# The opening of a windowed-attention and MoE kernel: two loads by SyncE in f32, a new order, normalisations on two engines

## The chip, the cores and the metric

The kernel runs on one NeuronCore of a Trainium2 chip. The metric is the device time of one execution in microseconds (us); lower is better. The core has five engines, each with its own queue of instructions that it works through in order: TensorE (PE, matmuls and weight loads), VectorE (DVE), ScalarE (ACT), GpSimd (POOL) and SyncE (SP, which only issues DMAs here). DMAs are moved by 16 DMA engines that all queues share. A DMA that POOL issues can change the type on the way (f32 to bf16); those that SP issues here keep it.

## The reference

```python
# q, k, v: [8, 8, 576, 64] f32
scores = scale * np.matmul(q, k.transpose(0, 1, 3, 2))
rel = pos[:, None] - pos[None, :]
mask = (rel >= 0) & (rel < 64)
scores = np.where(mask, scores, -1000000000.0)
attn = softmax(scores)                       # over the last axis
x = (attn @ v) laid out as [4608, 512]       # tokens x (heads x 64)
h = x @ w_in                                 # [512, 2048]
g = h * np.cos(h)
out = g @ w_out                              # [2048, 512]
```

Each token attends to itself and the 63 before it in its sequence. The result goes through a two-layer block with the gate h * cos(h).

## The kernel before

The 4,608 tokens are cut into 9 MoE tiles of 512 tokens. A tile's `h` is computed in 16 blocks of 128 features (4 matmuls of 512 columns each, L421), ACT takes the sine (cos(h) is sin(h + pi/2)), DVE multiplies (L549), and 4 blocks of 128 tokens of the result are summed over 16 matmuls each (L560). Attention for later tokens runs between these matmuls. All that is scheduled by hand: the program's order on each engine is the order in which the Python code emits its instructions.

Attention works on units (b, p, j): batch b, pair p of heads (two heads fill the 128 partitions), block j of 64 queries. Up to four units make a group. A group passes through these steps:

- load (`load_heads` L159: one pair of heads of q or k, 128 x 576, by POOL with a cast to bf16), transposes on PE through the identity (`transposed` L197, 18 matmuls of 64x64), and a copy from PSUM to `qT` or `kT` (`put_q` L217, `put_k` L242, DVE or ACT);
- scores (`g_scores` L262, PE; the first eight groups add the mask by a matmul with `mask16`, L270), the row maximum (`g_max` L292, DVE), the exponential with its sum (`g_exp` L304, ACT, four instructions of 128 columns), the reciprocal of the sum (`g_inv`, DVE, L318), the normalised weights `w` (`g_norm` L321, a product on POOL or DVE, L325);
- transposes of `w` (`g_trans` L328, on PE, or by a DMA of SP), their copy to `wT` (`g_put` L340), the product with v (`values_half` L364 for the first tile), the copy to `xT` (`put_x_half` L375).

`v` is needed with two alignments, so half of it is copied within SBUF (`spread_v` L180, by DVE, POOL, or a DMA of SP).

The opening, until the first tiles are under way, is the string `FIRST` (L47): a list of steps separated by blanks, which a loop (L524) emits one after the other. A step's first part names a function (the table `steps`, L505), the numbers are its arguments, and a last letter names the engine: d DVE, a ACT, p POOL, s SP. A number at the end of a step that writes PSUM picks one of five banks (`BANKS`, L121). The ones that matter here:

- `Lq0.p`, `Lk0.p`: load pair p of batch 0; `Lq1`, `Lk1` of batch 1; `Lv0`, `Lv1` chunks of v; `Lwi`, `Lwo` quarters of `w_in` and `w_out`. All of them are issued by POOL;
- `tq.p`, `tk.p` transposes and `pq.p`, `pk.p` copies of batch 0; `Tq`, `Tk`, `Pq`, `Pk` of batch 1;
- `s.p.g`, `m.p.g`, `e.p.g`, `i.p.g`, `n.p.g`, `w.p.g`, `c.p.g`: scores, maximum, exponential, reciprocal, normalisation, transposes and copy of group g of pair p; `Gs`, `Gm`, ... the same for later groups by their number;
- `v.a.g` and `x.a.g`: values and xT copy for pairs 2a, 2a+1 of half g of the first tile. `h.g.f`: 8 matmuls of 256 columns of the first tile's half g (`first_half` L380), `S` the sine, `g` the gate; `o` the second layer;
- `ms.i`: clear one of the eight `qB` tiles; `io`: an iota on POOL; `id`: the identity made from it on DVE (L138); `mk`: the masks on DVE (L140 to L149); `mc`: their cast on ACT; `zA`, `zB`, `zC`, `y`: pieces of `spread_v`; `tb`: ACT's table for the sine.

POOL's loads use eight semaphores in turn, so that each load waits for the landing of the one eight loads earlier; a load that waits holds up what stands behind it on POOL, products (`n...p`) among it. `h.0.0`, the first MoE matmuls, need `x.0.0` and `x.1.0`, and these need all four pairs' groups of half 0.

Of the kernel before, what the change touches and what calls it, by code (L numbers as in the profile page):

```python
# [10 lines left out]
def _safe_warn(msg, *a, **kw):  # L11
# [3 lines left out]
F32 = mybir.dt.float32  # L15
BF16 = mybir.dt.bfloat16
AF = mybir.ActivationFunctionType
ALU = mybir.AluOpType
# [18 lines left out]
RC = 9  # L37
PAIRS = 4
# [6 lines left out]


FIRST = (  # L47
# [21 lines left out]
)  # L69


# [1 line left out]
def kernel(  # L73
# [9 lines left out]
    nc = tc.nc  # L83
    B, H, S, D = q.shape
    assert (B, H, S, D) == (8, 8, 576, 64)
    scale = 1.0 / math.sqrt(D)
    d_model = H * D
# [10 lines left out]
    moe = ctx.enter_context(tc.tile_pool(name="moe", bufs=2))  # L98
# [10 lines left out]
    ident = const.tile([128, 128], BF16, name="ident")  # L109
    mask = const.tile([128, 3, 128], F32, name="mask")  # L110
# [4 lines left out]
    st = {}  # L115

    H_BANKS = [banks * 3 + ("X0",) for banks in (("O1", "X0", "X1", "S", "O0"), ("X0", "X1", "O1", "S", "O0"))]
    S_BANKS = ("X1", "S", "X0")  # L120
    BANKS = ("O1", "X0", "X1", "S", "O0")  # L121
    W_PARTS = 4
# [2 lines left out]
    def bank(which, name):  # L125
        return ps.tile([128, 512], F32, tag=which, name=name)

    def copy(engine, out, in_):
        {"a": nc.scalar.copy, "p": nc.gpsimd.tensor_copy}.get(engine, nc.vector.tensor_copy)(out, in_)  # L129
# [1 line left out]


    def put_steps():
        nc.gpsimd.iota(mask.rearrange("p u c -> p (u c)")[:, 0:192], pattern=[[1, 192]], base=0, channel_multiplier=-1,
                       allow_small_or_imprecise_dtypes=True)

    def put_ident():
        nc.vector.tensor_scalar(ident, mask[:, 0], 0.0, 1.0, ALU.is_equal, ALU.mult)  # L138

    def put_masks():  # L140
        steps = mask.rearrange("p u c -> p (u c)")
        for h in range(2):
            nc.vector.tensor_scalar(mask[64 * h:64 * h + 64, 2], steps[64 * h:64 * h + 64, 64 * h:64 * h + 128],
                                    2.0, -65.0, ALU.mult, ALU.add)
        nc.vector.tensor_tensor(out=mask[:, 2], in0=mask[:, 2], in1=mask[:, 2], op=ALU.mult)
        nc.vector.tensor_scalar(mask[:, 1], mask[:, 2], 64.0 ** 2, NEG, ALU.is_gt, ALU.mult)
        nc.vector.tensor_scalar(mask[:, 2], mask[:, 1], -1.0, NEG, ALU.mult, ALU.add)
        nc.vector.tensor_copy(mask[:, 0, 0:64], mask[:, 2, 0:64])
        nc.vector.memset(mask[:, 0, 64:128], NEG)  # L149
# [6 lines left out]
    def rows_tile(name):  # L156
        return ld.tile([128, NC * H * D], BF16, tag=name, name=name)

    def load_heads(name, b, p0=0, n=PAIRS):  # L159
        if (name, b) not in st:  # L160
            st[name, b] = rows_tile(name)[:, 0:PAIRS * RC * D].rearrange("p (a x) -> p a x", a=PAIRS)
        src = {"q": q, "k": k}[name][b, 2 * p0:2 * p0 + 2 * n]
        nc.gpsimd.dma_start(out=st[name, b][:, p0:p0 + n],
                            in_=src.rearrange("(a h) (p c) d -> (h p) a (c d)", h=2, c=RC))

    def load_chunk(name, b, c):
        if (name, b) not in st:
            st[name, b] = rows_tile(name)[0:NP].rearrange("p (c x) -> p c x", c=NC)
        src = {"q": q, "k": k}[name][b, :, c * NP:c * NP + NP]
        nc.gpsimd.dma_start(out=st[name, b][:, c].rearrange("p (h d) -> p h d", h=H),  # L170
                            in_=src.rearrange("h p d -> p h d"))
# [246 lines left out]
    def first(mt, ff, ks, start, stop):  # L418
        if start:
            st["h", ff] = bank(H_BANKS[mt == 1][ff], "h_ps")  # L420
        nc.tensor.matmul(out=st["h", ff], lhsT=w_in_sb[:, ks, ff * 128:ff * 128 + 128],  # L421
# [35 lines left out]
    n = n_listed  # L457
# [35 lines left out]
            at(time + 0.2 + 0.1 * p, put_x, mt, p, "a" if p == 1 else None)  # L493


    nc.vector.memset(small, 0.0)
    exp_table()

# [3 lines left out]
    def spread_first(lo, hi):  # L502
        return lambda i, engine: spread_v(0, i, engine, lo, hi)

    steps = {"Lq0": lambda p: load_heads("q", 0, p, 1), "Lk0": lambda p: load_heads("k", 0, p, 1),  # L505
             "Lq1": lambda p: load_heads("q", 1, p, 1), "Lk1": lambda p: load_heads("k", 1, p, 1),
             "Lv0": lambda c: load_v(0, c), "Lv1": lambda c: load_v(1, c), "Lq2": lambda c: load_chunk("q", 2, c), "Lk2": lambda c: load_chunk("k", 2, c),
             "Lwi": lambda i: load_w_in(i * d_ff // W_PARTS, (i + 1) * d_ff // W_PARTS),
             "Lwo": lambda i: load_w_out(i * n_ff // W_PARTS, (i + 1) * n_ff // W_PARTS),
             "io": put_steps, "id": put_ident, "mk": put_masks, "mc": cast_masks, "ms": clear_first,  # L510
             "tq": lambda p: tr_q(0, p), "tk": lambda p: tr_k(0, p), "Tq": lambda p: tr_q(1, p), "Tk": lambda p: tr_k(1, p),
             "pq": lambda p, engine: put_q(0, p, engine), "pk": lambda p, engine: put_k(0, p, engine),
             "Pq": lambda p, engine: put_q(1, p, engine), "Pk": lambda p, engine: put_k(1, p, engine),
# [16 lines left out]
    for mt in range(1, n_mt):  # L530
        base = mt * T
# [4 lines left out]
        for ff in range(n_ff):  # L536
# [8 lines left out]
            e = ff % 2  # L545
# [5 lines left out]
        for ms0 in range(0, MT // 128, 2):  # L551
            o_sb = moe.tile([128, 2, d_model], F32, tag="out", name="out_sb", bufs=2)
            o_ps = [bank(which, "out_ps") for which in (("O1",) if mt == n_mt - 1 and ms0 else ("O1", "O0"))]
            for e in range(2):
                ms = ms0 + e
# [44 lines left out]
```

## Time and profile before

| what | us |
|---|---|
| median of 3 runs | 317.94 (317.11 to 318.19) |
| the profiled execution's own time | 319.05 |
| its span (first to last instruction) | 317.3 |
| first transposes on PE | 4.53 |
| first exponential on ACT | 8.68 |
| first MoE matmul (L385) | 25.03 |
| PE busy in the span | 300.3 |

The profile is of one execution. Its times count from the first instruction. PEclk is the share of the TensorE clock that was granted. The timeline merges neighbouring instructions of one kind (x4: four of them) and gives in brackets how long the engine stood idle before, and what ended that.

The loads of the opening are issued by POOL from 1.25 us on and land one behind the other: q of the first pair (issued at 1.25) took 3.2 us to land, the next q (2.85) 4.5, the first quarter of w_in (12.93) 7.8 us.

### The profile page before, as it was taken

What the parts mean: (1) busy time and instruction counts of PE and PEld (TensorE: products, weight loads), DVE (VectorE), ACT (ScalarE), POOL (GpSimd) and SP (SyncE); (2) the same over time, 40 slices, a digit from 0 to 9 for tenths busy, and PEclk for the clock granted to TensorE, in tenths of its full rate; (3) what the DMA queues carried; (4) which work ended last, traced back from release to release, by engine and by line L of the source; (5) the groups of instructions that cost most, each with busy time, mean ns of one, the idle gap of its engine ahead of it and who ended that gap; (6) DMA issues with size and microseconds to landing.
All of it is one profiled execution on the core that took longest, in us unless ns stands there. A gap on an engine that the chain in (4) does not pass through costs nothing.

```text
span 317.3 us, 7950 instructions
## 1 busy us (share of the span) xinstructions
PE 300.3 (95%) x2627; PEld 163.4 (51%) x2659; DVE 233.4 (74%) x879; ACT 236.5 (75%) x784; POOL 192.7 (61%) x226
## 2 busy tenths in 40 slices
PE   3859999999999999899999999999999999999995
PEld 2747864544554555445554555555455554454443
DVE  5996998779867985598769875978699758435811
ACT  3977689686997699669986998699968996215600
POOL 7879648994469687968688878797842640000000
PEclk9987999999999999999999999999999999999999
DMA  6999999999959995999979997999793433011011
GB/s 89 183 209 161 191 187 154 121 147 138 259 93 104 136 227 74 119 130 230 125 90 143 218 117 94 126 211 154 89 141 138 82 73 132 0 68 66 1 66 68
DMA packets 155162, 40.88 MB, mean 129 GB/s; under 512 B 143280, under 2 KB 150640, under 8 KB 155120
## 3 DMA queue, kind: packets, MB, share of 16 engines
q0 software_dynamic: 100480, 18.36, 81.3%
q1 hardware_dynamic: 54496, 21.81, 37.2%
q8 instruction: 21, 0.34, 0.5%
q14 instruction: 21, 0.17, 0.2%
q10 hardware_dynamic: 144, 0.20, 0.2%
HBM read 36.70 MB, written 9.44 MB: 145 GB/s over the span
## 4 chain that ended last, share of the span: by engine, by line
PE 62%; ACT 14%; DVE 14%; DMA 5%; issue 3%; POOL 2%; DVEq 0%; POOLq 0%; ACTq 0%
PE h_ps L421 26%; PE out_ps L560 21%; ACT e L311 11%; DVE gT L549 6%; PE h_ps L385 5%; DVE s L300 2%; DMA out_dram<-out_sb 2%; DVE qB L129 2%; PE o_ps L352 2%; PE s_ps L280 2%; PE out_ps L404 2%; DMA k<-in_k_dram 2%; DVE v L129 1%; POOL w L325 1%; PE tq_ps L207 1%
## 5 line engine op out<-in xcount | busy, mean ns | idle before, releaser
L421 PE MATMUL h_ps<-xT,w_in 128*128 128x512 bf16 x498 | 115.5, 379 | 1.7 <-ACT xT L129 0.7
L560 PE MATMUL out_ps<-w_out,gT 128*128 128x512 bf16 x482 | 116.1, 379 | 0.8 <-issue 0.2
L546 ACT ACTIVATE sin<-h_ps 128x512 f32<-128x512 f32 x128 | 74.2, 599 | 35.4 <-PE h_ps L421 32.5
L311 ACT ACTIVATE e<-s,negm 128x128 f32<-128x128 f32 x256 | 99.1, 400 | 1.4 <-DVE negm L300 1.2
L549 DVE TENSOR_TENSOR gT<-h_ps,sin 128x512 bf16<-128x512 f32 x128 | 81.5, 686 | 21.3 <-ACT sin L546 20.6
L325 POOL TENSOR_TENSOR w<-e,rden 128x512 bf16<-128x512 f32 (+1 forms) x75 | 71.5, 963 | 39.2 <-DVE rden L318 29.6
L421 PEld LDWEIGHTS <-w_in 128*128 128x128 bf16 x512 | 48.5, 98 | 54.9 <-issue 1.7
L560 PEld LDWEIGHTS <-gT 128*128 128x128 bf16 x496 | 45.9, 98 | 44.2
L300 DVE CUSTOM_DVE_ANT_0 s<-s_ps,mask 128x128 f32<-128x128 f32 x256 | 58.2, 286 | 1.3 <-PE s_ps L286 1.0
L311 ACT ACTIVATION_READ_ACCUMULATOR e<-s,negm 128x1 f32 x256 | 51.0, 199 | 0.0
L170 POOL DMA_DIRECT2D q<-in_q_dram x36 | 28.9, 803 | 11.7 <-DMA q<-in_q_dram 6.9
L176 POOL DMA_DIRECT2D v<-in_v_dram x40 | 34.1, 870 | 0.4 <-DMA q<-in_q_dram 0.4
L170 POOL DMA_DIRECT2D k<-in_k_dram x36 | 28.5, 793 | 5.3 <-DMA k<-in_k_dram 3.7
L318 DVE RECIPROCAL rden<-den 128x4 f32<-128x4 f32 (+1 forms) x79 | 13.7, 174 | 20.9 <-ACT e L311 19.4
L129 ACT COPY out_sb<-out_ps 128x512 f32<-128x512 f32 (+1 forms) x18 | 10.4, 577 | 24.8 <-PE out_ps L560 18.7
L129 DVE COPY out_sb<-out_ps 128x512 f32<-128x512 f32 x18 | 12.4, 690 | 16.4 <-PE out_ps L560 12.0
L280 PEld LDWEIGHTS <-qB 128*128 128x128 bf16 x216 | 17.0, 98 | 14.3 <-DVE negm L300 0.4
L129 DVE CAST xT<-o_ps 128x512 bf16<-128x512 f32 x24 | 15.5, 679 | 9.5 <-PE o_ps L352 9.5
L280 PE MATMUL s_ps<-kT,qB 128*128 128x128 bf16 x216 | 21.9, 219 | 0.0
L129 DVE COPY qB<-tq_ps 64x576 bf16<-64x576 bf16 x48 | 21.6, 451 | 0.3
L300 DVE DVE_READ_ACCUMULATOR2_ANT negm<- 128x1 f32 x256 | 21.4, 83 | 0.0
L129 POOL COPY v<-v 64x1536 bf16<-64x1536 bf16 (+1 forms) x10 | 16.8, 1684 | 5.0 <-DMA v<-in_v_dram 4.7
(62 smaller groups left out, 260.5 us busy)
## 6 DMA issues: line engine op xcount, KB each, us to landing
out_dram<-out_sb SPq DMA_DIRECT2D x16, 512.0 KB, 7.8
v<-in_v_dram POOLq DMA_DIRECT2D x32, 128.0 KB, 6.0
q<-in_q_dram POOLq DMA_DIRECT2D x36, 96.0 KB, 8.8
k<-in_k_dram POOLq DMA_DIRECT2D x36, 96.0 KB, 8.8
w_in<-in_moe_w_in_dram POOLq DMA_DIRECT2D x4, 512.0 KB, 8.8
w_out<-in_moe_w_out_dram POOLq DMA_DIRECT2D x4, 512.0 KB, 10.8
q<-in_q_dram POOLq DMA_DIRECT2D x8, 144.0 KB, 5.8
k<-in_k_dram POOLq DMA_DIRECT2D x8, 144.0 KB, 6.0
```

Source lines behind the costliest of these rows:

```text
L129: {"a": nc.scalar.copy, "p": nc.gpsimd.tensor_copy}.get(engine, nc.vector.tensor_copy)(out, in_)
L170: nc.gpsimd.dma_start(out=st[name, b][:, c].rearrange("p (h d) -> p h d", h=H), in_=src.rearrange("h p d -> p h d"))
L176: nc.gpsimd.dma_start(out=vt.rearrange("p (h d) -> p h d", h=H), in_=v[b, :, c * 128:c * 128 + n, :].rearrange("h p d -> p h d"))
L280: nc.tensor.matmul(out=s_ps[:, u].rearrange("p (a t) -> p a t", a=2), lhsT=qblocks[(b % 2) * PAIRS + p][:, j].rearrange("d h t -> d (h t)" ...
L300: nc.vector.tensor_tensor_reduce(out=s[:, u], in0=s_ps[:, u], in1=mask[:, 2 - j % 2 if j else 0], scale=-scale if b else -1.0, scalar=BIG, ...
L311: nc.scalar.activation(e[:, u], s[:, u], AF.Exp, bias=negm[:, u:u + 1], scale=1.0 if n < n_first else -1.0, accum_out=den[:, u:u + 1])
L325: (nc.gpsimd if engine == "p" else nc.vector).tensor_tensor(out=w[:, 0:u], in0=e[:, 0:u], op=ALU.mult, in1=rden[:, 0:u].unsqueeze(2).to_br ...
L385: nc.tensor.matmul(out=h_ps[:, half * e:half * e + half], lhsT=w_in_sb[:, ks, ff * 128:ff * 128 + 128], rhs=st["xT", 0][:, ks, half * g:ha ...
L421: nc.tensor.matmul(out=st["h", ff], lhsT=w_in_sb[:, ks, ff * 128:ff * 128 + 128], rhs=st["xT", mt][:, ks], start=start, stop=stop)
L546: nc.scalar.activation(sin, h_ps, AF.Sin, bias=math.pi / 2.0)
L549: nc.vector.tensor_tensor(out=gt[:, e], in0=h_ps, in1=sin, op=ALU.mult)
L560: nc.tensor.matmul(out=o_ps[e], lhsT=gT[ff // 2][:, ff % 2, ms * 128:ms * 128 + 128], rhs=w_out_sb[:, ff], start=ff == 0, stop=ff == n_ff - 1)
```

## The change

- q and k of the first pair of heads are loaded by SP, as f32, into a spare tile (`load_plain`), and cast to bf16 on DVE (`cast_plain`, steps `cq.d` and `ck.d`). Before, POOL loaded them with the cast.
- The identity is made by a helper on POOL (a clear and a select, ahead of everything else) in place of one DVE instruction; the masks' step pattern comes from two iotas of 64 x 128 on POOL, in place of one of 128 x 192 and two instructions of DVE.
- The list `FIRST` is another one. POOL's order of loads is now q and k of pairs 1 to 3 of batch 0, q and k of pair 0 of batch 1, four chunks of v, q of pair 1 of batch 1, then w_in; k of pair 1 of batch 1 comes after most of w_in. Of the eight first groups' normalisations, three are on DVE (`n.0.0.d`, `n.3.0.d`, `n.1.1.d`), where all were on POOL; the two pieces `zA` of v's copy are on POOL, where they were on DVE; the copy `y.1` goes from DVE to a DMA of SP; four of the eight copies `c` of the first groups are on ACT, where one was. Before `h.0.0`, PE has three of the batch 1 transposes (four before), and the later groups 8, 9, 10 (before: 9, 10, 11, 12).
- One entry of the second tile's bank order is changed.

```diff
 FIRST = (
-    "ms.0.d Lq0.0 Lk0.0 ms.1.d ms.2.d io id tq.0 mk Lq0.1 mc pq.0.d Lk0.1 tk.0 pk.0.a s.0.0.0 Lq0.2 tq.1 "
-    "tk.1 m.0.0 pq.1.a ms.3.d s.0.1.1 Lk0.2 tq.2 pk.1.d s.1.0.2 Lq0.3 Lk0.3 tk.2 s.1.1.3 e.0.0 tq.3 "
...
-    "e.1.1 w.0.0 zA.0.d w.1.0 c.0.0.d Gs.12.0 w.2.0 n.3.0.p i.0.1 c.1.0.d zA.1.d c.2.0.d e.2.1 zB.0.s "
-    "zB.1.s n.0.1.p i.1.1 w.3.0 v.0.0 c.3.0.d x.0.0.a s.3.1.3 Gm.10 v.1.0 m.3.1 i.2.1 Gs.11.2 Gm.9 Gm.12 "
-    "n.1.1.p x.1.0.a e.3.1 ms.4.d w.0.1 w.1.1 c.1.1.a i.3.1 h.0.0.1 h.0.1.4 tb n.2.1.p c.0.1.d Lwi.3 "
...
+    "ms.0.d Lq0.0 Lk0.0 io Lq0.1 Lk0.1 ms.1.d ms.2.d Lq0.2 Lk0.2 ms.3.d mk cq.d ck.d Lq0.3 Lk0.3 tq.0 "
+    "ms.4.d mc pq.0.a tk.0 pk.0.d Lq1.0 tq.1 s.0.0.0 pq.1.d tk.1 s.0.1.1 pk.1.a m.0.0 Lk1.0 e.0.0 m.0.1 "
+    "s.1.1.2 Lv0.0 m.1.1 s.1.0.3 m.1.0 tq.2 pq.2.d e.0.1 tk.2 tq.3 pk.2.d Lv0.1 e.1.0 tk.3 Lv0.2 pq.3.d "
+    "pk.3.a Lv0.3 zB.0.s s.2.0.4 Tq.0 Lq1.1 i.0.0 i.1.0 s.2.1.0 Lwi.0 Tk.0 m.2.0 s.3.0.1 Gs.8.3 e.1.1 "
+    "e.2.0 Pq.0.d n.1.0.p Lwi.1 Pk.0.d m.3.0 Gs.9.2 e.3.0 Gs.10.4 n.0.0.d w.1.0 Lwi.2 i.2.0 zA.0.p w.0.0 "
+    "m.2.1 s.3.1.1 i.3.0 c.1.0.a e.2.1 n.2.0.p w.2.0 c.2.0.a n.3.0.d zA.1.p c.0.0.d w.3.0 i.0.1 v.0.0 "
+    "x.0.0.a c.3.0.d ms.5.d n.0.1.p m.3.1 i.2.1 v.1.0 Tq.1 Gm.10 x.1.0.a w.0.1 e.3.1 i.1.1 h.0.0.0 "
...
-    H_BANKS = [banks * 3 + ("X0",) for banks in (("O1", "X0", "X1", "S", "O0"), ("X0", "X1", "O1", "S", "O0"))]
+    H_BANKS = [banks * 3 + ("X0",) for banks in (("O1", "X0", "X1", "S", "O0"), ("X0", "O1", "X1", "S", "O0"))]
...
     def put_steps():
-        nc.gpsimd.iota(mask.rearrange("p u c -> p (u c)")[:, 0:192], pattern=[[1, 192]], base=0, channel_multiplier=-1,
-                       allow_small_or_imprecise_dtypes=True)
-
-    def put_ident():
-        nc.vector.tensor_scalar(ident, mask[:, 0], 0.0, 1.0, ALU.is_equal, ALU.mult)
+        for h in range(2):
+            nc.gpsimd.iota(mask[64 * h:64 * h + 64, 0], pattern=[[2, 128]], base=-65, channel_multiplier=-2,
+                           allow_small_or_imprecise_dtypes=True)
 
     def put_masks():
-        steps = mask.rearrange("p u c -> p (u c)")
-        for h in range(2):
-            nc.vector.tensor_scalar(mask[64 * h:64 * h + 64, 2], steps[64 * h:64 * h + 64, 64 * h:64 * h + 128],
-                                    2.0, -65.0, ALU.mult, ALU.add)
-        nc.vector.tensor_tensor(out=mask[:, 2], in0=mask[:, 2], in1=mask[:, 2], op=ALU.mult)
+        nc.vector.tensor_tensor(out=mask[:, 2], in0=mask[:, 0], in1=mask[:, 0], op=ALU.mult)
...
+    def load_plain(name):
+        rows = moe.tile([128, 2, d_model], F32, tag="out", name="rows", bufs=2).rearrange("p a f -> p (a f)")[:, 0:RC * D]
+        st["rows", name] = rows
+        nc.sync.dma_start(out=rows, in_={"q": q, "k": k}[name][0, 0:2].rearrange("h (p c) d -> (h p) (c d)", c=RC))
+
+    def cast_plain(name, engine):
+        if (name, 0) not in st:
+            st[name, 0] = rows_tile(name)[:, 0:PAIRS * RC * D].rearrange("p (a x) -> p a x", a=PAIRS)
+        copy(engine, st[name, 0][:, 0], st.pop(("rows", name)))
...
+    make_identity(nc, ident)
     nc.vector.memset(small, 0.0)
     exp_table()
...
-    steps = {"Lq0": lambda p: load_heads("q", 0, p, 1), "Lk0": lambda p: load_heads("k", 0, p, 1),
+    steps = {"Lq0": lambda p: load_heads("q", 0, p, 1) if p else load_plain("q"),
+             "Lk0": lambda p: load_heads("k", 0, p, 1) if p else load_plain("k"),
+             "cq": lambda engine: cast_plain("q", engine), "ck": lambda engine: cast_plain("k", engine),
...
-             "io": put_steps, "id": put_ident, "mk": put_masks, "mc": cast_masks, "ms": clear_first,
+             "io": put_steps, "mk": put_masks, "mc": cast_masks, "ms": clear_first,
```

30 rows, old and new, of the table FIRST are left out of this document.

## The prediction

> **What bounds the kernel now.** I read the page first: its busy times, then its 40 slices.
>
> ```profile
> span 317.3 us, 7950 instructions
> PE 300.3 (95%) x2627; PEld 163.4 (51%) x2659; DVE 233.4 (74%) x879; ACT 236.5 (75%) x784; POOL 192.7 (61%) x226
> PE   3859999999999999899999999999999999999995
> ```
>
> PE is idle for 317.3 - 300.3 = 17 us, and nearly all of it lies in the first four slices of 7.9 us: from there on PE sets the pace. So a change of the opening is worth the PE idle time (and the slowly clocked PE time) that it takes out before the dense part begins, less the PE work that it leaves for later. Next the table of windows (length, then busy us of PE, PEld, DVE, ACT, POOL, each with its count, PE clock, DMA share, GB/s):
>
> ```profile
> 4.50:10.80 6.30, 5.76 (x118) 4.35 (x120) 4.05 (x9) 3.95 (x14) 5.07 (x9) 1.00 1.11 161
> 10.80:17.00 6.20, 4.74 (x186) 3.92 (x182) 5.91 (x13) 6.18 (x32) 5.72 (x8) 1.00 1.85 175
> 17.00:21.03 4.03, 1.94 (x26) 1.39 (x26) 3.90 (x7) 3.92 (x21) 3.38 (x4) 1.00 1.27 207
> 21.03:27.90 6.87, 6.28 (x68) 4.76 (x69) 6.03 (x37) 4.71 (x14) 4.97 (x6) 0.50 1.03 177
> 27.90:34.00 6.10, 6.10 (x85) 5.14 (x84) 4.19 (x8) 3.79 (x7) 4.60 (x8) 1.00 1.18 181
> ```
>
> PE is starved at 17-21 us, then runs at half clock for 6.87 us, and is full from 27.9 us. Before 10.8 us the record says 1.00, but 18 transposes took 0.69 us there and 0.44 after, so that stretch is slow too. The timeline (start, us, engine, line, op) shows who starves it:
>
> ```profile
> 2.85 0.58 POOL L163 DMA_DIRECT2D q<-in_q_dram  x1
> 4.53 0.69 PE L204 MATMUL tq_ps<-ident,q 64*64 64x64 bf16 x18 [4.53 <-DMA q<-in_q_dram]
> 8.68 0.36 ACT L311 ACTIVATE e<-s_ps,negm 128x128 f32<-128x128 f32 x1
> ...
> 15.69 4.04 POOL L325 TENSOR_TENSOR w<-e,rden 128x512 bf16<-128x512 f32 x4
> 17.71 2.17 DVE L129 COPY v<-v 64x512 bf16<-64x512 bf16 x1
> 20.63 0.93 DVE L129 COPY v<-v 64x512 bf16<-64x512 bf16 x1
> 22.19 0.59 ACT L129 CAST xT<-o_ps 128x512 bf16<-128x512 f32 x1 [1.27 <-PE o_ps L371]
> 23.75 0.59 ACT L129 CAST xT<-o_ps 128x512 bf16<-128x512 f32 x1 [0.97 <-PE o_ps L371]
> 25.03 3.29 PE L385 MATMUL h_ps<-xT,w_in 128*128 128x256 bf16 x16
> ```
>
> PE waits 4.53 us for the first load. ACT makes its first exponential at 8.68 and then works almost without pause. Four normalisations run one behind the other on POOL (15.69-19.73), and the two copies of v on DVE, which stand on the chain of waits at 17.80 and 20.63, last 2.17 and 0.93 us although their work is small. The first MoE matmul (L385) can start only at 25.03, after the second xT copy ends at 24.34. This start is the figure I follow.
>
> **Change, part by part.** Durations are rows of before.
>
> *First load.* SyncE has nothing to do until 18.16, so its two issues can leave at about 0.8 us, when the other engines start. Landing: bounds 2.0 us (a late 256 KB store on idle DMA engines) and 7.6 (a 512 KB store under load); I take POOL's own first load, 3.24 us from issue, also on idle engines: landed by 4.1. That is hidden by DVE, which meets its casts only after four clearings (0.97 + 4 x 0.583 = 3.30) and the mask steps (3.75 to 4.86 before, so 1.11): 4.41. With the cover gone a landing at 8.4 would cost 4 us. A cast of 576 f32 columns has no row: 0.23 (128 columns, L138) to 0.75 (576 out of PSUM); from the 0.20 of 64 and 0.23 of 128 columns in SBUF, 0.5 ns a column, I take 0.46. PE starts at 4.87, 0.34 *later* than before; k's cast hides behind q's transposes. With 0.75 it is 0.63 later.
>
> *Identity and masks on POOL.* The identity's clear and select and two iotas now stand ahead of q0.1's issue. Each costs at least 0.10 (a memset row) and at most 1.04 (a 512-column product); near the iota row, 0.34, with a short memset, I take 1.3 for all: issue at about 2.2, against 2.85 before. It landed 4.5 us after issue as the third in the queue, and 3.24 is the row for the first: 5.4 to 6.7, I take 6.1. DVE loses the identity (0.23) and two mask steps (0.59); that is counted in the 4.41's slack, since the 1.11 begins at the later product.
>
> *First exponential.* The new list puts q0.1's transposes ahead of the first scores on PE, and k0.1's transposes and copy ahead of the first exponential on ACT. At the slow clock: q and k transposed by 4.87 + 2 x 0.70 = 6.27; kT copied by DVE (0.75) at 7.05 while q0.1 is transposed (until 7.0); scores 1.0, 8.05; k0.1's transposes 0.69, 8.75; its copy on ACT 0.65: 9.40. That is 0.72 later than 8.68.
>
> *ACT's chain to the second xT copy.* Seven steps of four exponentials, 1.45 each (12.74 to 14.2 is one): 10.15; kT 0.67; two wT copies taken over from DVE, 0.61 each; two xT copies, 0.59 each: 13.2. A wait of 0.35 for DVE, whose queue of reductions (0.69) and copies (0.75) reaches the sixth maximum 0.35 late: 13.6. End: 9.40 + 13.6 = 23.0. Before, 8.68 to 24.34 = 15.66, with waits of 1.27 and 0.97 for o_ps. These go because v's copies move to POOL and half the products to DVE (0.69 by L325's DVE rows). The copies there cost 0.64 (POOL rows 1894 and 1477 ns for 2048 and 1536 columns, so 0.815 ns a column and 0.22) and end before the second xT by 0.7 us in my chain.
>
> *Start of h and what is left over.* h starts at 23.05: 25.03 - 23.05 = **1.98 gained**. But by then PE has not yet done what before had: one k transpose (0.45), one step of w transposes (0.40) and 6 score matmuls (28 less 22; 14 took 0.58, so 0.25): **1.10 given back**. In the dense part this is paid in full.
>
> *Loads.* With two fewer loads ahead of them on POOL's queue, and q1.1 alone ahead of w_in, w_in's first quarter, 20.77 before, cannot be later than h's 23.05 unless the queue stands still: no cost; if it came 3 us later, 0.7.
>
> *Later list.* DVE's 64x2048 copy of v (1.14 at 53.80, followed on the chain of waits by a POOL product and PE's transposes) goes to SyncE. Bound: none to 0.4 us of gain (11 matmuls of 0.216 took 2.76, not 2.4); I take **0.2**. The moved and re-banked groups there cost nothing under PE, or up to 0.5 if one bank is late.
>
> *Clock.* PE rests at 17-22 us in the new list too: half clock for about as long as before, taken as no change.
>
> Sum: -1.98 + 1.10 - 0.2 = **-1.1 us**. The profiled execution's own time is 319.05 (1.75 around its span of 317.3); it would be about 318.0. Against the runs' median of 317.94 it gives **316.9 us**.
>
> **Rivals.**
>
> *A, late second heads (slower).* Place: PE's and ACT's queues before the first scores. Every us by which q0.1 lands after 6.3 goes whole into h's start, as ACT's chain has no slack behind it; the sum is spent at 7.4, so it decides from there. For it: before, it landed at 7.36, and the product before it in the list (first scores) did not wait for it. If POOL's pieces take 1.04 each (issue at 4.05) and the load 4.5: 8.55, 2.25 late: 317.94 - 1.1 + 2.25 = 319.1. Against: an empty queue and the short iota row.
>
> *B, the clock never falls (faster).* Half clock cost before, from 25.03 to 27.86, half of 2.83 = 1.4 us. PE's busy share in the starved stretch rises from 1.94/4.03 = 48% to some 70% (about 3.5 us of transposes, scores and values in 17.8-22.8). 4.74/6.20 = 76% at 10.8-17 us did not drop the clock. If 70% is enough: 316.9 - 1.4 = 315.5. Against: the clock did fall after 48%, and no row lies between. [...]
>
> *C, DVE and POOL shut each other out.* The 64x512 copy took 2.17 us at 17.71, while POOL's products ran until 19.72, and 0.93 at 20.63, while one ran until 21.41: it ends about 0.15 after POOL, so DVE waited. DVE's 384-column product at 56.09 ended 0.41 after POOL's did. With products on both engines the third and fourth meet POOL's product and copies and end up to 1.0 later; my chain has 0.7 of slack for them, and the second v copy adds 0.6: 0.9 us. 316.9 + 0.9 = 317.8, no change. [...]
>
> **Chances and range.** Forecast 45%, A 28%, B 15%, C 12%. About 0.3% (0.95 us) is what a measurement of this kernel can tell from no change, and the forecast lies just past it: of its 45, faster 25, same 16, slower 4. A: slower 25, same 3. B: faster 15. C: faster 2, same 5, slower 5. Faster 0.42, same 0.24, slower 0.34. Range: down to B with 0.5 for the later list, 315.0; up to A with 0.4 for a slow cast (0.63 - 0.34 = 0.3) and a bank: 319.5. The forecast's own range is 315.9 to 318.0.
>
> **What would show it.** [...] A first exponential past 10.5 makes A right; a granted clock of 1.00 throughout makes B right; DVE products that end with POOL's make C right. The prediction is wrong if the time after 45 us moves by more than the opening did, or if SyncE's loads land after 4.4.

## The result: slower by 1.2%, and the profile after

| | before | after |
|---|---|---|
| median (range) | 317.52 (316.88 to 318.19) | 320.77 (319.55 to 322.27) |
| ratio, 95% interval | | 1.0121 (1.0084 to 1.0157) |
| the profiled execution, and its span | 319.05, 317.3 | 321.01, 319.2 |
| first exponential / first MoE matmul | 8.68 / 25.03 | 9.38 / 21.82 |
| first matmul of the second layer (L404, now L408) | 42.86 | 39.63 |
| second tile's first layer starts (L421, now L425) | 62.36 | 65.61 |

Medians take every run of a kernel; ratios and their intervals leave out the runs that lie over 1.5% above the fastest of the same kernel, up to three here, so a ratio need not be the quotient of the medians.

The change made the opening earlier by 3.2 us, and this lead was still whole at 40 us. Then it was lost twice over: the second tile starts 3.25 us later than before. That this is also the difference of the medians (3.25) is in part chance. The two profiled executions differ by only 1.96, since the one of before lost more time in its third tile, most of it in one wait for transposed weights:

```profile
128.24 0.55 PE L352 MATMUL o_ps<-wT,v 128*64 128x64 bf16 x20 [1.50 <-DMA wT<-w]
```

The page of the changed kernel shows the place in two rows:

```profile
span 319.2 us, 7952 instructions
...
PE 298.0 (93%) x2627; PEld 162.3 (51%) x2659; DVE 229.7 (72%) x875; ACT 236.2 (74%) x786; POOL 191.5 (60%) x227
...
PE   3879998399999999999999989999999999999996
...
PEclk9999999699999999999999999999999999999999
```

The third slice (16 to 24 us), which had a 5 before, now has a 7. But the eighth (55.9 to 63.8) fell from 9 to 3, and the granted clock there from 9 to 6. The opening, in the timeline:

```profile
4.37 0.54 DVE L129 CAST q<-rows 128x576 bf16<-128x576 f32 x1
...
4.97 0.69 PE L208 MATMUL tq_ps<-ident,q 64*64 64x64 bf16 x18 [4.97 <-DVE q L129]
...
6.78 0.69 PE L208 MATMUL tq_ps<-ident,q 64*64 64x64 bf16 x18 [0.58 <-DMA q<-in_q_dram]
...
9.38 0.37 ACT L315 ACTIVATE e<-s_ps,negm 128x128 f32<-128x128 f32 x1
...
18.64 1.03 DVE L329 TENSOR_TENSOR w<-e,rden 128x512 bf16<-128x512 f32 x1
...
20.54 1.33 ACT L129 CAST xT<-o_ps 128x512 bf16<-128x512 f32 x2
...
21.82 1.36 PE L389 MATMUL h_ps<-xT,w_in 128*128 128x256 bf16 x11
```

The copies to xT now stand on ACT without a wait in brackets. And the stretch of the loss, by windows (length, busy us of PE, PEld, DVE, ACT, POOL, then PE clock, DMA share, GB/s), before and after:

```profile
56.00:60.00 4.00, 3.86 (x41) 1.96 (x39) 2.84 (x9) 3.08 (x13) 4.00 (x6) 1.00 1.11 98
60.00:64.00 4.00, 3.84 (x69) 2.20 (x69) 2.66 (x11) 2.30 (x8) 4.00 (x6) 1.00 2.00 137
```

```profile
56.00:60.00 4.00, 0.00 (x0) 0.00 (x0) 0.85 (x2) 0.00 (x0) 2.00 (x4) 0.74 1.77 105
60.00:64.00 4.00, 3.07 (x46) 1.62 (x48) 0.00 (x0) 0.59 (x2) 2.56 (x4) 0.50 1.93 132
```

PE and ACT stand still at 56-60 us and DVE nearly, while the transfers go on. The chain of waits (start, us, what) names one:

```profile
46.36 0.93 POOL w L329
47.29 13.59 DMA v<-in_v_dram
60.88 0.04 issue
60.93 0.64 PE o_ps L356 x10
61.56 1.82 PE out_ps L408 x4
```

This is chunk 4 of v of batch 0 (64 rows, `Lv0.4`), which the first values of the second tile (`V.1`) need. Before, it was issued at 52.58, landed at 56.88 and was first used at 58.61, so there was 1.7 us to spare. Now it was issued 5.3 us earlier and landed 4 us later. The granted clock falls in this wait of 5.93 us too: 0.5 from 57.93 to 64.75 us. Its name is not yet its cause, though, since several transfers land near 60 us.

The view of the DMA queues, for the same 10 us (48-58) of before and after, shows the load. The digits are the busy tenths of the 16 engines in 40 slices:

```profile
DMA  9999999997999999999999299999999999970005
...
DMA packets 7411, 1.44 MB, mean 144 GB/s; under 512 B 7217, under 2 KB 7409, under 8 KB 7409
```

```profile
DMA  9999999999999999999999999899999999999999
...
DMA packets 6672, 1.47 MB, mean 147 GB/s; under 512 B 6221, under 2 KB 6669, under 8 KB 6669
```

Both move about the same bytes. Before, the engines run dry at 57 us; after, they do not in this stretch. SyncE's order is another one, too. Before, its copy of v (issued at 52.39) stands behind the transposes of groups 12 and 11 (49.65 and 51.07); after, there are two copies (46.23 and 48.74), and both stand ahead of the transposes of group 11 (49.42). The stream of loads is no earlier than before: the last of w_out and of batch 1's v had both landed by 48.56 before and by 48.63 after, although PE is 3.2 us ahead.

### The profile page after: what moved, and what is told of

It is laid out like the page before. It is cut to its first block, busy times and chain, and to the rows that moved or that the text cites. A ratio compares the mean times of both kernels' runs of the same rounds, so it can differ in the third digit from the quotient of the medians.

```text
span 319.2 us, 7952 instructions
## 1 busy us (share of the span) xinstructions
PE 298.0 (93%) x2627; PEld 162.3 (51%) x2659; DVE 229.7 (72%) x875; ACT 236.2 (74%) x786; POOL 191.5 (60%) x227
## 4 chain that ended last, share of the span: by engine, by line
PE 69%; DMA 12%; ACT 5%; SPq 4%; POOL 4%; issue 2%; DVE 2%; DVEq 0%; POOLq 0%
PE h_ps L425 30%; PE out_ps L567 29%; ACT e L315 4%; DMA v<-in_v_dram 4%; DMA w_out<-in_moe_w_out_dram 4%; PE s_ps L284 3%; PE o_ps L356 3%; DMA out_dram<-out_sb 3%; SPq L244 2%; SPq L341 2%; PE tq_ps L211 2%; DMA q<-in_q_dram 2%; POOL w L329 2%; PE out_ps L437 1%; PE out_ps L408 1%
## 5 line engine op out<-in xcount | busy, mean ns | idle before, releaser
L425 PE MATMUL h_ps<-xT,w_in 128*128 128x512 bf16 x498 | 115.4, 379 | 1.5 <-ACT xT L129 0.4
L553 ACT ACTIVATE sin<-h_ps 128x512 f32<-128x512 f32 x128 | 74.4, 598 | 35.6 <-PE h_ps L425 33.3
L329 POOL TENSOR_TENSOR w<-e,rden 128x512 bf16<-128x512 f32 (+1 forms) x73 | 69.5, 961 | 29.3 <-DVE rden L322 23.2
L425 PEld LDWEIGHTS <-w_in 128*128 128x128 bf16 x512 | 48.7, 98 | 54.6 <-issue 1.2
L315 ACT ACTIVATION_READ_ACCUMULATOR e<-s,negm 128x1 f32 x256 | 48.0, 188 | 0.0
L129 ACT COPY out_sb<-out_ps 128x512 f32<-128x512 f32 (+1 forms) x17 | 9.6, 563 | 24.9 <-PE out_ps L567 18.7
L129 DVE COPY out_sb<-out_ps 128x512 f32<-128x512 f32 x19 | 13.1, 690 | 16.2 <-PE out_ps L567 12.0
L129 POOL COPY v<-v 64x1536 bf16<-64x1536 bf16 (+2 forms) x12 | 18.3, 1526 | 5.4 <-DMA v<-in_v_dram 5.0
```

The costliest lines, as they stand in the source:

```text
L315: nc.scalar.activation(e[:, u], s[:, u], AF.Exp, bias=negm[:, u:u + 1], scale=1.0 if n < n_first else -1.0, accum_out=den[:, u:u + 1])
L329: (nc.gpsimd if engine == "p" else nc.vector).tensor_tensor(out=w[:, 0:u], in0=e[:, 0:u], op=ALU.mult, in1=rden[:, 0:u].unsqueeze(2).to_br ...
L553: nc.scalar.activation(sin, h_ps, AF.Sin, bias=math.pi / 2.0)
```

## The experiments

All were run beside the kernel before, whose medians in the five calls lay between 316.87 and 317.67. "Landed" and "start" come from one profiled execution each, which need not be typical: those of e7, e9 and e14 were the fastest of their kernels (316.77, 318.64, 314.56), and that of e8 lies 3.0 us under its median. Edits are steps of `FIRST`; "second tile" is the start of its first layer.

**Is it that one load?** (e1, and e3 as its control)

```diff
-Lwo.3 Lq2.0
+Lwo.3 Lv0.4 Lq2.0
...
-Ge.13 Lv0.4 Gn.11.p
+Ge.13 Gn.11.p
```

> Chunk 4 of v of batch 0 is issued straight after w_out's last quarter (some 38 us) instead of at 47.29 us; nothing else moves. Theory ONE LOAD: its landing at 60.88 us is all that PE waited for. Then the idle 5.93 us before the first values of the second tile goes, and with it the half clock at 57.93-64.75 us, which cost half of the 3.8 us of PE time behind 60.93: 320.8 - 5.9 - 1.9 = 313.0, with small new waits 313 to 314.5, granted clock 1.00 throughout. Rival WHOLE QUEUE: everything that the DMA engines carry at 43-62 us is late in the changed kernel; the same values also need the transposed weights of groups 12 and 11, which SyncE's transposes delivered only at 55.97 and 60.5 us, so PE stops there instead, until 59 to 60.5: 318.5 to 320.5, with the half clock still there.

> The kernel before with the same move of chunk 4 of v (issued before the first q chunk of batch 2). There it landed at 56.88 and was first used at 58.61, so ONE LOAD gives no change: 317.5 within 0.9. If it is faster by over 1 us, the load's place cost something before too that the trace hides; if slower, moving it pushes the q chunks of batch 2 or the transposes by SyncE.

e1: 320.88, ratio to before 1.0131 (1.0088 to 1.0174), nothing gained. The load was early, and PE stood as long for the next transfer, the transposed weights of group 11. In PE's timeline of e1:

```profile
54.44 0.22 PE L356 MATMUL o_ps<-wT,v 128*64 128x64 bf16 x2
60.57 0.59 PE L356 MATMUL o_ps<-wT,v 128*64 128x64 bf16 x14 [5.91 <-DMA wT<-w]
```

ONE LOAD has fallen. e3 (317.71, ratio 1.0037, 1.0008 to 1.0066) gained nothing either; if anything it lost a little, so the load's old place was no fault.

**Do the copies of v crowd the transposes?** e2 puts `y.1` back on DVE, e4 (and again e14) both `y.0` and `y.1`; e15 is the kernel before with both on DVE, e6 the kernel before with both by SyncE.

```diff
@@ e2 @@
-y.1.s
+y.1.d
@@ e4, e14 @@
-y.0.s
+y.0.d
...
-y.1.s
+y.1.d
@@ e6, in the kernel before @@
-y.1.d
+y.1.s
@@ e15, in the kernel before @@
-y.0.s
+y.0.d
```

> The second copy of v of batch 1 goes back from a DMA of SyncE to DVE, as before the change. Theory COPIES CROWD: SyncE's two copies (1024-byte packets, 46.23 to 57.57 us) slow POOL's loads; without one of them chunk 4 of v lands by 58 us, PE's idle time there falls from 5.9 to under 3, time 316 to 318. Rival BACKLOG: POOL's loads were late before the copies began (w_out's last quarter landed at 48.63 against 46.04); chunk 4 lands at 60 to 61 as before, PE waits as long, and DVE's copy of 1.14 us is added or hidden: 320 to 322.

> Both copies of v of batch 1 on DVE, none by SyncE. COPIES CROWD: chunk 4 of v lands by 57 us, the idle time before the second tile's values is under 2 us, 315 to 317 with up to 1.1 us for DVE's copies. BACKLOG: chunk 4 lands after 59.5, PE idle over 4 us, 319 to 322.

> The kernel before with one part of the change alone: the copy y.1 of v by a DMA of SyncE in place of DVE. The prediction gave this a gain of 0.2 (317.0). DMA-BOUND: its 256 packets of 1,024 bytes take the place of other packets among the transposes; without the second copy the changed kernel's transposes landed about 3 us earlier; here the loads' queue has run dry by 53 us, so part is hidden: 317.5 to 319.5, with the later transposes landing 1 to 2.5 us after 57.57.

> The changed kernel with both copies of v of batch 1 on DVE, a second time, since 316.6 then was 0.4% under the kernel before with an interval that just reached 1. If it is really faster: 315.5 to 317 and an upper bound of the ratio under 1. If the medians of kernels with PE this close behind the transposes wander with the landing of them, as 318.24, 318.63 and 317.63 of its three relatives suggest: 317 to 318.5, no difference from before.

> The kernel before with its one SyncE copy of v of batch 1 (y.0) on DVE as well: the control for the runs with both copies on DVE. There PE comes 3.5 us later and everything has landed by 57.57, before V.1 at 58.61 uses it: no change, 316.5 to 317.8, or up to 1.1 slower for DVE's copy if DVE has no room. If it gains 1 us or more, the copies cost something in the kernel before too.

| run | median | ratio (95%) | chunk 4 landed | groups 11 / 13 landed | second tile |
|---|---|---|---|---|---|
| after | 320.77 | 1.0121 (1.0084 to 1.0157) | 60.88 | 60.50 / 62.64 | 65.61 |
| e2 | 319.44 | 1.0074 (1.0036 to 1.0112) | 56.23 | 57.47 / 61.52 | 62.78 |
| e4 | 316.60 | 0.9961 (0.9921 to 1.0001) | 54.65 | 56.44 / 59.63 | 60.88 |
| e14 | 316.58 | 0.9987 (0.9952 to 1.0022) | 54.21 | 56.11 / 59.26 | 60.52 |

Copy by copy the transposes land earlier and the loss goes. With both copies back the intervals are clear of after's; e2's overlaps it, and e2 is still slower than before, so `y.1` alone is not shown to be the whole loss. e2's waits were as COPIES CROWD said (0.81, 1.01 and 0.59 us), its time was not. e6 puts `y.1` alone into the kernel before: 318.27, ratio 1.0042 (1.0013 to 1.0071), last transposes landed at 60.84 instead of 57.57 (3.3 us later, where 1 to 2.5 was expected), and PE waits there, 0.24 us for the copy and 0.50 for the transposes. e15 shows that one copy alone cost the kernel before nothing: 317.16, ratio 0.9984 (0.9949 to 1.0018). e4's gain over before did not hold when it was repeated: e4 and e14 equal the kernel before.

**Whose queue, or whose engines?** e10 lets ScalarE issue the two copies; e9 leaves them with SyncE and issues the six k chunks of batch 2 later.

```diff
@@ e10 @@
-y.0.s
+y.0.A
...
-y.1.s
+y.1.A
...
-        if engine == "s":
-            nc.sync.dma_start(out=to, in_=of)
+        if engine in ("s", "A"):
+            (nc.scalar if engine == "A" else nc.sync).dma_start(out=to, in_=of)
@@ e9, Lk2.0 to Lk2.3 taken out of their places ahead of V.1 @@
-V.1 Gn.17.p X.1.a o.2.3 Gp.15.d Lk2.4 Gp.16.d Lk2.5 V.3
+V.1 Gn.17.p X.1.a Lk2.0 Lk2.1 Lk2.2 Lk2.3 Lk2.4 Lk2.5 o.2.3 Gp.15.d Gp.16.d V.3
```

> The changed kernel with the two copies of v of batch 1 issued by ScalarE in place of SyncE: same packets, another queue. DMA-BOUND: the packets share the 16 engines whoever issues them; group 11's transposes land at 59.5 to 61 and chunk 4 of v as late, 320 to 322. Rival ONE BEHIND THE OTHER: SyncE's transposes were late because they stood behind the copies in SyncE's own queue; then group 11 lands by 57.5, near 56.44 as without copies, chunk 4 of v still near 60, and with ScalarE's two issues (0.6 us each) 318.5 to 320.5.

> The changed kernel with one thing moved: the six k chunks of batch 2 are issued only behind V.1 (from some 60 us, before from 49.02). The copies of v stay with SyncE. If the loads beside them are what slows the transposes (DMA-BOUND), group 11's transposes land at 57 to 59 instead of 60.5 and chunk 4 of v at 57 to 60 instead of 60.88: 318 to 320. Rival COPIES ONLY: the k chunks stand behind chunk 4 in POOL's queue and do not matter: both land at 60 to 61 again, 320 to 321.5.

e10: 320.21, ratio 1.0116 (1.0075 to 1.0157). Group 11 did land early (56.62), as ONE BEHIND THE OTHER said, and so did chunk 4 (55.56). Its time lies in both expected ranges and decides nothing. But now the copy itself was last:

```profile
55.61 0.22 PE L356 MATMUL o_ps<-wT,v 128*64 128x64 bf16 x2 [1.41 <-DMA v<-in_v_dram]
56.66 0.25 PE L356 MATMUL o_ps<-wT,v 128*64 128x64 bf16 x4 [0.83 <-DMA wT<-w]
60.53 0.48 PE L356 MATMUL o_ps<-wT,v 128*64 128x64 bf16 x10 [3.62 <-DMA v<-v]
```

Three kernels, three different last transfers, one time: chunk 4 at 60.88 (after), group 11 at 60.52 (e1), a copy at 60.40 (e10). That fits a fixed end of the sum of what the engines carry for `V.1`, not of any one of its parts: the order inside only says which part is last. This is a reading of three executions; no run issues the copies by SyncE behind the transposes.

e9 takes other work out of the same sum: 319.77, ratio 1.0115 (1.007 to 1.0161). Group 11 landed at 58.72 and chunk 4 at 56.90, as DMA-BOUND expected, and the second tile started at 63.15 in the profile; the median moved by 1.0 against after, less than the intervals tell apart.

**Less of it all.** e5: both copies on DVE, chunk 4 early, k chunks late. e16: three of the q chunks late too. e11 and e12: copies on DVE, chunk 4 early, `V.0` before `V.1`, in e12 with three k chunks late.

```diff
@@ e5, on top of e4; Lv0.4 and Lk2.0 to Lk2.3 taken out of their old places @@
-Lwo.3 Lq2.0
+Lwo.3 Lv0.4 Lq2.0
...
-X.1.a o.2.3 Gp.15.d Lk2.4 Gp.16.d Lk2.5 V.3
+X.1.a Lk2.0 Lk2.1 Lk2.2 Lk2.3 Lk2.4 Lk2.5 o.2.3 Gp.15.d Gp.16.d V.3
@@ e16, on top of e5; Lq2.3, Lq2.4 and Lq2.5 taken out of their old places @@
-Gn.14.d o.3.0
+Gn.14.d Lq2.3 o.3.0
...
-oc.0.d Ge.16
+oc.0.d Lq2.4 Ge.16
...
-Gn.13.p o.2.2
+Gn.13.p Lq2.5 o.2.2
@@ e11, on top of e4; Lv0.4 as in e5 @@
-V.1 Gn.17.p X.1.a o.2.3
+V.0 Gn.17.p X.0.a o.2.3
...
-V.3 V.0
+V.3 V.1
...
-X.3.a X.0.a
+X.3.a X.1.a
@@ e12, on top of e11; Lk2.3 taken out of its old place @@
-Gp.15.d Lk2.4 Gp.16.d Lk2.5 V.3 V.1
+Gp.15.d Gp.16.d V.3 Lk2.3 Lk2.4 Lk2.5 V.1
```

> The changed kernel with less for the DMA engines to move before the second tile's values: both copies of v of batch 1 on DVE, the six k chunks of batch 2 issued only behind V.1 (from some 56 us, before from 49.02), chunk 4 of v issued behind w_out's last quarter. Theory DMA-BOUND: from 26 to 62 us the DMA engines never run dry, and PE, 3.2 us earlier, overtakes them; the transposes of groups 11, 14 and 13, which landed at 56.44, 58.61 and 59.63 without the copies, come 2 to 4 us earlier without the k chunks beside them; PE idle at 50-62 us under 1.5, clock 1.00 throughout, 313.5 to 315. Rival TRANSPOSES ALONE: SyncE's transposes are slow whatever runs beside them; group 11 lands at 56 to 57 again and the time stays at 316 to 317.

> The kernel with less for the DMA engines (label e5_light_dma), and the last three q chunks of batch 2 issued some 4 to 6 us later too, so that the transposes run beside fewer loads. DMA-BOUND: groups 11, 14 and 13 land by 55 to 56 (56.72, 56.90 and 57.40 there), V.1 waits under 0.5 and the second tile starts at 58 to 59; q of batch 2 is then the next to be late, its transposes due some 1 us into the second tile: 316 to 317.5. Rival: q late costs PE more than it gains, 318 to 320.

> The changed kernel with both copies of v of batch 1 on DVE, chunk 4 of v early, and the second tile's values in the order in which their transposes land (pair 0 first, pair 1 third). In the kernel with both copies on DVE alone PE stood 0.98 for group 11 and 1.15 for group 13. If these waits are what is left, the first goes: the second tile's first layer starts at 59.5 to 60.5 (60.88 there), 315 to 316.5. Rival: the last transposes (group 13 at 59.6) set it anyway, no gain over the 316.6 of that kernel.

> The same with the last three k chunks of batch 2 behind the values of pair 3. DMA-BOUND: group 13 lands 0.5 to 1.5 us earlier than in the kernel of the same call with the chunks in place (label e11_y_dve_v0_first), the second tile starts by as much earlier, 314.5 to 316. Rival: the late chunks make k of batch 2 late in the second tile, as the run with all six late (318.24) may have shown: 317 to 318.5.

e5: 318.24, ratio 1.0021 (0.9989 to 1.0052), slower than both theories expected. Group 11 landed at 56.72, no earlier than in e4, as TRANSPOSES ALONE said. Groups 14 and 13 did land earlier (56.90 and 57.40), and its DMA engines run dry as before the change. For 48-58 us of e5:

```profile
DMA  9999999999999999999991599905990000110289
...
DMA packets 5892, 1.10 MB, mean 110 GB/s; under 512 B 5888, under 2 KB 5888, under 8 KB 5888
```

The second tile started at 59.82, 2.5 us before the kernel before. Yet the total gained nothing: the second tile took 33.3 us instead of 32.3, with a wait for transposed weights at its end, probably because other loads moved to where they meet these. e16 shows that strongest: second tile at 59.42, but 35.8 us long, 2.63 us of it one wait for transposed weights at 94.74; 318.06, ratio 1.0037 (1.0004 to 1.007). Its group 11 landed at 55.15, as expected, but groups 14 and 13 at 57.21 and 58.17, later than in e5. e11 (318.63, 1.0021, 0.9981 to 1.0062) and e12 (317.63, 1.0014, 0.998 to 1.0047) missed the times expected: group 13 landed at 60.95 and 60.49, and PE stood 3.70 and 2.64 us for it. None of these orders gained anything.

**What the opening is worth.** e7 is e5 with the first q and k loaded by GpSimd; e8 is e5 with all eight normalisations on GpSimd.

```diff
@@ e7, the same for Lk0; the steps cq.d and ck.d go @@
-    steps = {"Lq0": lambda p: load_heads("q", 0, p, 1) if p else load_plain("q"),
+    steps = {"Lq0": lambda p: load_heads("q", 0, p, 1),
@@ e8 @@
-n.0.0.d
+n.0.0.p
...
-n.3.0.d
+n.3.0.p
...
-n.1.1.d
+n.1.1.p
```

> The kernel with less for the DMA engines (label e5_light_dma), its first two heads' q and k loaded by GpSimd with the cast, as before the change; no casts on DVE. If SyncE's loads are what makes the opening earlier: two more loads stand ahead of q of the second pair, which then lands 0.8 to 1.5 later than 6.73, the first exponential comes at 10 to 10.9 instead of 9.38, and the first MoE matmul 0.7 to 1.5 after e5's: 0.5 to 1.5 us slower than e5. If the opening's gain comes from the later steps alone: PE's first transposes come at 4.6, a little earlier than 4.97, nothing else moves, within 0.4 of e5.

The "one or two windows" of half clock expected of e8 are 3.41 or 6.83 us: the granted clock was at half for 3.41 us in the profile of e12, for 6.83 in those of before and after, and for 10.24 in that of e1.

> The same kernel (label e5_light_dma) with all eight normalisations of the first half on GpSimd: three products of about 1 us go back from DVE to GpSimd's queue, which also makes the copies zA. If sharing them is what filled PE before the first MoE matmul: second xT copy 1.5 to 3 us later than 21.87, PE starved at 17 to 22 us, and the granted clock falls to half for one or two windows: 2 to 4 us slower than e5. Rival: ACT's chain of exponentials sets the start anyway; under 0.7 us slower and clock 1.00.

e7: 319.29, ratio 1.0068 (1.0035 to 1.0102), 1.05 above e5 by the medians; the two intervals overlap. q of the second pair landed at 7.33, the first exponential came at 10.24 (e5: 9.05), the first MoE matmul at 22.81 (21.49). So the loads by SyncE are worth 1.2 to 1.3 us of the lead in these executions. e8: 322.10, ratio 1.0114 (1.0061 to 1.0167), 3.9 above e5 by the medians and some 3 by the ratios. The second xT copy ends at 22.78, 0.9 after 21.87 and so less late than the 1.5 to 3 expected; the first MoE matmul comes at 23.05, 1.56 after e5's, and the clock falls for 6.83 us. Its windows, and those of after for the same stretch:

```profile
17.00:21.00 4.00, 2.55 (x32) 1.69 (x29) 1.19 (x5) 3.70 (x18) 3.94 (x6) 0.79 1.16 177
21.00:28.00 7.00, 6.80 (x87) 5.43 (x86) 5.12 (x26) 5.03 (x14) 5.57 (x8) 0.63 0.82 147
```

```profile
17.00:21.00 4.00, 2.83 (x61) 2.12 (x62) 3.15 (x8) 4.00 (x20) 2.83 (x4) 1.00 1.21 200
21.00:28.00 7.00, 6.87 (x121) 5.56 (x115) 6.86 (x35) 6.90 (x19) 6.37 (x10) 1.00 1.16 197
```

With three products on DVE, GpSimd's busy time at 17-21 us is 2.83 instead of 3.94, ACT does not wait at all (4.00 of 4.00), and PE keeps its clock. It does not always: in the profile of e12, whose opening is the same list, the clock fell for 3.41 us from 19.36 on.

**What the clock costs.** e13 puts 24 matmuls that compute nothing needed ahead of `V.1`; e17 combines both copies on DVE with two fillers of five; e18 puts fillers into the opening of the kernel before.

```diff
@@ e13 @@
-Gi.17 V.1
+Gi.17 fill V.1
...
+    def fill():
+        f_ps = bank("O0", "f_ps")
+        for i in range(24):
+            nc.tensor.matmul(out=f_ps, lhsT=w_in_sb[:, 0, 0:128], rhs=w_out_sb[:, 0], start=i == 0, stop=i == 23)
@@ e17, on top of e4 @@
-V.1 Gn.17.p
+fill.5 V.1 Gn.17.p
...
-V.2 X.2.d
+fill.5 V.2 X.2.d
@@ e18, in the kernel before, bank X0 @@
-e.1.1 w.0.0
+e.1.1 fill.3 w.0.0
...
-i.1.1 w.3.0 v.0.0
+i.1.1 fill.4 w.3.0 fill.3 v.0.0
```

> The changed kernel with 24 matmuls of 512 columns (0.216 us each, 5.2 in all) put on PE straight ahead of V.1, into a bank that nobody reads: they lie in the 5.9 us of waiting, so that the wait stays and the clock has no reason to fall. If the loss is wait plus half clock: granted clock 1.00 throughout, the second tile starts 1.5 to 2 us earlier than 65.61, 318.7 to 319.5. If the clock's fall cost nothing there (the stretch after the wait is paced by the transposes that land later): 320.3 to 321.3.

> The changed kernel with both copies of v of batch 1 on DVE and two short fillers of five 512-column matmuls (1.08 us each) on PE, ahead of V.1 and of V.2, into a bank that nobody reads. Without fillers its runs were at 316.58, 5 of 12 of them with a granted clock of 0.995 or less. If PE's idle time ahead of the second tile now only costs through the clock: clock 1.00 in all runs, 315 to 316.3, faster than before with its interval. If the fillers delay the values more than the clock gives: 316.6 to 317.5.

> The kernel before with ten matmuls of 512 columns (2.16 us) on PE in the gaps at 16.8 to 21.6 us, into a bank that nobody reads, so that PE rests less there. The prediction priced the half clock of the opening (rival B) at 1.4 us. If that price is right: clock 1.00 in most runs, 315.2 to 316 against 316.9. If the fillers only delay the values (they lie on the chain to the first MoE matmul) or the clock falls all the same: 316.5 to 318.

e13: 317.20, ratio 1.0021 (0.9988 to 1.0053), with the clock at 1.00 in all 12 runs; after, it was 0.989 in all four. PE's timeline of e13:

```profile
54.68 5.34 PE L510 MATMUL f_ps<-w_out,w_in 128*128 128x512 bf16 x23
59.96 0.55 PE L356 MATMUL o_ps<-wT,v 128*64 128x64 bf16 x16
60.44 1.04 PE L408 MATMUL out_ps<-w_out,gT 128*128 128x512 bf16 x4
...
63.65 0.59 PE L425 MATMUL h_ps<-xT,w_in 128*128 128x512 bf16 x2
```

The values still begin at 59.96, but four matmuls of the second layer then take 1.04 us (1.82 by the chain of after), and the second tile starts at 63.65, 1.96 before after's 65.61. That is the 1.5 to 2 expected. The medians differ by 3.6, more than that: after's PE was also idle for 1.00 and 0.63 us in its fifth and sixth tile (0.24 in e13's); in the fifth PE's longest wait is for a maximum of DVE, and DVE's own longest one is 2.4 us for a store. Whether these hang on the clock was not tried. In e13, whose transfers are those of after, chunk 4 landed at 56.37 and group 11 at 60.01: with the same transfers either can be last, and the end near 60 stays.

In the profile of after the clock fell at 57.93, 2.9 us into the wait of 5.93, and stayed at 0.50 for 6.83 us. In e13, with 5.34 us of fillers in place of the wait, it stayed at 1.00.

e17: **315.91, ratio 0.9959 (0.9927 to 0.9991), the only kernel of the study whose interval lies under 1**, and 4.9 us under after. It was not repeated, and the like ratio of e4 did not hold when that was. Its fillers end when the values' data are there, and no wait is left at `V.1` or `V.2`:

```profile
55.44 1.24 PE L509 MATMUL f_ps<-w_out,w_in 128*128 128x512 bf16 x5
56.61 0.44 PE L355 MATMUL o_ps<-wT,v 128*64 128x64 bf16 x16
...
58.58 1.25 PE L509 MATMUL f_ps<-w_out,w_in 128*128 128x512 bf16 x5
59.76 0.62 PE L355 MATMUL o_ps<-wT,v 128*64 128x64 bf16 x16
```

The second tile starts at 61.19, no earlier than in e4 and e14 (60.88 and 60.52). The clock was under 0.998 in 3 of its 12 runs, where none was expected, against 5 of e14's 12; the gain over e14, 0.7 us by the medians, is smaller than the intervals tell apart. e18 says nothing on the clock. Its bank was still being read by exponentials, and PE, which works in order, stood for it:

```profile
21.04 0.59 PE L505 MATMUL f_ps<-mask,ident 128*128 128x512 bf16 x1 [4.25 <-ACT e L311]
```

The first MoE matmul came at 28.09 and the time was 322.57, ratio 1.0118 (1.0054 to 1.0182). So no edit isolates the price of the opening's half clock. The runs of the kernel before in the five calls show it as a correlation: 35 of them had a mean granted clock of 0.998 or more and averaged 316.57 us; 29 had 0.987 to 0.989, as in its profile with 6.83 us at half clock, and averaged 318.11. The difference, 1.54, is close to the 1.4 of rival B.

## Why the prediction was wrong

- *First load*: right. Landed at 3.69 (by 4.1), cast 0.54 (0.46), transposes at 4.97 (4.87).
- *Identity and masks on POOL*: q of the second pair was issued at 1.75 (2.2) and landed at 6.73 (6.1); the load took 4.98, more than the 3.9 chosen, and less than the 7.4 from which rival A decides.
- *First exponential*: 9.38 against 9.40.
- *ACT's chain*: mis-sized by 1.1. It ends at 21.87 (23.0), 12.49 after the first exponential instead of 13.6. The wait of 0.35 for DVE did not come: ACT was busy 4.00 of 4.00 us at 17-21. And a step of four exponentials took 1.38 from start to start, not 1.45, which is 0.5 over seven steps. The start of h was therefore 3.21 earlier, not 1.98.
- *Clock*, "taken as no change": wrong in the opening, where rival B's event came and the clock stayed at 1.00. e8 shows that the shared normalisations kept it up, though not in every execution (e12). Over the whole run the clock was halved for 6.83 us in both profiles, at 21.03-27.86 before and at 57.93-64.75 after; that the two are equal is luck, as the step meant the opening. With B's own price and the PE work left over, -3.21 - 1.4 + 1.10 = -3.5; the first matmul of the second layer was 3.23 earlier. The terms fit together, but neither was isolated.
- *Loads*: the step asked only whether w_in came in time, which it did. It did not ask what the later loads would meet.
- ***Later list*: the step that failed**, and with it the premise ahead of all parts, "from there on PE sets the pace", by which a lead of the opening lasts to the end. *Later list* gave y.1 by SyncE a gain of 0.2 and let the rest cost "nothing under PE, or up to 0.5". In place of that the second tile started 3.25 us late after a lead of 3.2: some 6.5 us were lost on the way, in a wait for transfers of 5.93 us and the half clock behind it. The page of before spoke against the premise, as "nearly all" was misread: of PE's 17 us of idleness 9.2 lie in the first four slices and 4.6 between 31.7 and 309.4 us. A copy taken from DVE is added to DMA engines that are busy until 57 us: alone, in the kernel before, it cost 0.4% (e6), and taken out of the changed kernel with its sister it gave 4.2 us back (e4, and e14 again). But e14, with its lead whole and both copies on DVE, only equals the kernel before (0.9987), so the lead too was worth nothing. A lead of 3.2 us is larger than the 1.7 us by which chunk 4 was early before, and the loads had not become any earlier. Of the loss, about 2 us at the start of the second tile were the clock (e13).
- *Rivals*. A did not happen (the first exponential came before 10.5), though the sign was its own. C may show in one row, DVE's product of 1.03 us at 18.64, beside a copy of v on GpSimd (18.52 to 19.13): the products at 16.30 and 23.07 took 0.68. It delayed nothing, the one at 16.30 also ran beside a copy of GpSimd (16.56 to 17.45), and no run shows that the two engines shut each other out. None of the three placed anything past 30 us; the sentence on what would make the prediction wrong, that the time after 45 us moves by more than the opening did, is what came true.

What stays open: how the loss divides between the copy, the lead and the rest of the later list, since no run joins the new opening to the old later list; why the lead is worth nothing in e5 beyond the waits named there, since medians of kernels that run this close behind their transfers wander by a us or two; and what sets the pace of the engines in this stretch, packets, bytes or the mix of both. Loads alone went at 1,189 packets a us and 158 GB/s (before, 46 to 48 us); loads, copies and transposes together at 525 packets and 143 GB/s (after, 52 to 58 us), and from 58.4 to 59.4 us at only 9 to 13 GB/s, for a reason that the trace does not show.

## What to carry to other kernels

Before a change brings one stage forward, look up for the next stage how early each transfer it needs had landed (here 1.7 us), and whether the DMA engines run dry before it: a lead larger than that can become a wait. If taking one late transfer away only makes another one last at the same time, stop reordering and take work out of the sum. A long wait on PE can be paid twice, once itself and once through the clock behind it (here 5.93 us, and about 2 more); a few idle matmuls in its place, into a bank that is surely free, can save the second payment.

## What the hardware showed that was not expected

- SyncE's transposes of 128 x 512 took 7.4 to 11.1 us from issue to landing beside a full queue of GpSimd's loads, and 3.1 to 5.6 in the kernel before, whose queue was shorter then: GpSimd's loads issued at 45 to 61 us took 3.9 to 5.4 us there, and up to 13.97 after the change.
- The stretches at half clock were 3.41, 6.83 or 10.24 us long (e12, after, e1). In the 3.41 us ahead of the fall at 21.03 before, PE was busy for 1.94 us. But the clock stayed at 1.00 behind 3.41 us with 1.86 of them busy (before, 126.40 to 129.81) and with 1.79 (after, 15.04 to 18.45), so the busy time alone does not tell when it falls.
